# Routing's intermediates in the PSUM bank of the logits, and some of routing's copies on ScalarE, in an attention and mixture-of-experts kernel

## The chip, the cores and the metric

The kernel runs on one core of a Trainium2 chip. The core has five engines that run side by side, each through its own list of instructions in order: TensorE (PE in the profile; PEld are its weight loads), VectorE (DVE), ScalarE (ACT), GpSimd (POOL) and SyncE (SP), which here issues most of the DMAs. They hand work to each other through semaphores. There are two on-chip memories of 128 partitions: SBUF, and PSUM with eight banks, into which TensorE writes its results. The metric is the device time of one execution in microseconds. Lower is better.

## The reference

An attention over 64 heads (8 batches of 8 heads, 576 tokens, head size 64) that keeps only the keys whose score lies within `tau` of the row's maximum, followed by a mixture of 8 experts, of which each token uses the one with the largest logit:

```python
scores = scale * np.matmul(q, k.transpose(0, 1, 3, 2))
thresh = np.max(scores, axis=-1, keepdims=True) - tau
scores = np.where(scores >= thresh, scores, -1000000000.0)
attn = np.exp(scores - np.max(scores, axis=-1, keepdims=True))
attn = attn / (np.sum(attn, axis=-1, keepdims=True) + 1e-09)
x = np.matmul(attn, v)            # then (4608 tokens, 512)
logits = x @ w_gate               # (4608, 8)
expert_idx = np.argmax(logits, axis=1)
probs = softmax(logits)           # with 1e-09 added to the sum
out[n] = probs[n, e] * (np.maximum(x[n] @ w1[e], 0.0) @ w2[e])   # e = expert_idx[n]
```

## The kernel before, in words

The heads are worked on in 32 pairs, four pairs to a batch. For each pair the scores are computed twice: once with queries on the partitions (`s_unit`), where VectorE takes the row maxima out of PSUM (L288), and once with keys on the partitions (`st_unit`), with the threshold of each row already subtracted by TensorE (the operand CQ, L325). ScalarE takes the exponential of the second (L341), VectorE masks it by the sign of the score (L344), ScalarE casts it to 16 bits (L349) and GpSimd computes the remainder of that cast (L350). The product with the values follows (`av_piece`). All numbers go through TensorE as pairs of 16-bit values, high and low part; the low parts of queries and keys are made by L209, those of the values by L243, both on VectorE.

The row maxima of a pair go through TensorE as a transpose (L299, the tile pst), are split into three 16-bit rows (L304 to L307, the tile ptT) and are copied by DMA into CQ (L312).

When the four pairs of a batch are done, `finish` divides by the row sums (rs: L422, L423, for the half-filled tile of odd batches also L427, L428), GpSimd multiplies (L437), and the 16-bit rows are written into R, the rows that will be sent to the experts. `logits` has TensorE compute the logits (the tile lg). VectorE adds their high and low parts into the SBUF tile L (L470), and `route` works on that: the maximum mx, a one-hot oh of the first largest expert by way of w, rank8 and mw, and the difference ex. The nested `ranks` has TensorE count in a second tile rk, by two triangular matmuls, how many tokens of this and the earlier batches go to the same expert; VectorE makes of it the row posi to which each token is sent (L517, L520, L522, L524), and of ex the weight of its expert (L519 to L525). `run` holds the counts so far, `was` its copy from before this batch, `tid` the tokens' numbers. GpSimd sends each row of R by an indirect DMA (L534) to the table xs in HBM. The experts fetch their rows from xs, and TensorE computes them (L777, L804), for the most part after the attention.

Three things set the order of the work. A planner in the code counts steps, eleven to a pair of heads, and runs functions at a step and at one of three places in it, FRONT, MID and END; `after(k, f)` plans f k steps later, and `chain(k, fs)` spreads a list of functions over MID and END of successive steps. The tile framework then puts every engine's instructions into a fixed list, by readiness and the order of the program, with a timeline of its own (`schedule_with_timeline_sim=True`). And tiles are taken from pools: a tile of a pool with one buffer is given out again only when every reader of the last one is done. This one matters here:

```python
ps_m = ctx.enter_context(tc.tile_pool(name="ps_m", bufs=1, space=bass.MemoryType.PSUM))   # L67
ps = ps_m.tile([P, 512], F32, tag="m", name=f"pst_{n}")    # the transposes of the row maxima
lg = ps_m.tile([P, 512], F32, tag="m", name=f"lg_{b}")     # the logits
rk = ps_m.tile([P, 512], F32, tag="m", name=f"rk_{b}")     # the ranks
pc = ps_m.tile([P, 512], F32, tag="m", name=f"pc_{nm}")    # the counts for the tables, three times
```

All four share one bank of PSUM, one after the other. The logits use 64 or 80 of its 512 columns, the ranks 32 or 40.

The functions that the diff touches:

Of the kernel before, what the change touches and what calls it, by code (L numbers as in the profile page):

```python
# [50 lines left out]
def kernel(  # L51
# [355 lines left out]

    R = rpool.tile([P, 5, ROW], I32, name="R")
    Rf = R.bitcast(F32)
    L = rpool.tile([P, 5, E], F32, name="L")  # L410


    def finish(b):
        x = str(b) if b >= B - 3 else ""
        gap, lag, dist = (TUNE[z + x] for z in "gld")
        off = TUNE["off" + x] if b < B - 1 else 2
        n = NT + b % 2
        x4, xh = x_tiles(b)
        rs = small.tile([P, 5, H], F32, tag="rs", name=f"rs_{b}", bufs=2)
        eps = 1e-9 * SV / SX  # L420
        fs = [
            lambda: nc.vector.tensor_scalar(rs[:, 0:NT].unsqueeze(3), x4[:, :, :, D:W], eps, None, ALU.add),  # L422
            lambda: nc.vector.reciprocal(rs[:, 0:NT], rs[:, 0:NT]),  # L423
        ]
        if n > NT:
            fs += [
                lambda: nc.vector.tensor_scalar(rs[:, NT].unsqueeze(2), xh[:, :, D:W], eps, None, ALU.add),  # L427
                lambda: nc.vector.reciprocal(rs[:, NT], rs[:, NT]),  # L428
            ]
        chain(0, fs)  # L430
        xTs = {}

        def one(j):
            xr = x4[:, j] if j < NT else xh
            x = xp.tile([P, DM], F32, tag="xn", name=f"xn_{b}_{j}", bufs=2).rearrange("p (h d) -> p h d", h=H)
            eng = nc.vector if (b, j) in XV else nc.gpsimd
            eng.tensor_tensor(  # L437
                x, xr[:, :, 0:D], rs[:, j].unsqueeze(2).to_broadcast([P, H, D]), ALU.mult
            )
            x = x.rearrange("p (c u) d -> p c (u d)", c=4)  # L440
            Rv = R[:, j, 0:DM].bitcast(F16).rearrange("p (c h d) -> p c h d", c=4, h=2)

            def high():
                nc.scalar.copy(Rv[:, :, 0, :], x)
                eng.tensor_tensor(Rv[:, :, 1, :], x, Rv[:, :, 0, :], ALU.subtract)
                after(lag, turn)

            def turn():
                if j % 2 == 0:
                    xTs["t"] = rpool.tile([P, 2, 8, P], F16, tag="xT", name=f"xTg_{b}_{j}", bufs=3)  # L450
                xTs[j] = xT = xTs["t"][:, j % 2]
                nc.sync.dma_start_transpose(xT, R[:, j, 0:DM].bitcast(F16))

            after(lag, high)

        for j in range(n):
            after(off + gap * j, lambda j=j: one(j))
        after(off + gap * (n - 1) + 2 * lag + TUNE["lg7" if b == B - 1 else "lg"], lambda: logits(b, n, xTs, dist))

    def logits(b, n, xTs, dist):  # L460
        lg = ps_m.tile([P, 512], F32, tag="m", name=f"lg_{b}")
        lv = lg[:, 0:n * 2 * E].rearrange("p (j h e) -> p j h e", j=n, h=2)
        seq = [(0, 0)] + [(c, 1) for c in range(4)] + [(c, 0) for c in range(1, 4)]
        for j in range(n):
            for m, (c, h) in enumerate(seq):
                nc.tensor.matmul(
                    lv[:, j, 0:2 - h], xTs[j][:, 2 * c + h, :], wg[:, c, 0:2 - h, :],
                    start=(m == 0), stop=(m == 7),
                )
        after(1, lambda: nc.vector.tensor_reduce(  # L470
            L[:, 0:n, :], lv.rearrange("p j h e -> p j e h"), axis=AX.X, op=ALU.add
        ), FRONT)
        after(TUNE["route"], lambda: route(b, n, dist))

    def route(b, n, dist):

        Lj = L[:, 0:n, :]
        bc = [P, n, E]

        def t3(nm, dt=F32):  # L480
# [2 lines left out]
        def t2(nm, dt=F32):  # L483
            return small.tile([P, 5, 1], dt, tag=nm, name=f"{nm}_{b}", bufs=2)[:, 0:n, :]

        tt = nc.vector.tensor_tensor
        mx, w, mw, oh, ex, ps, pos, sm = (
            t2("mx"), t3("w"), t2("mw"), t3("oh", F16), t3("ex"), t3("ps"), t2("pos"), t2("sm")
        )
        was = small.tile([P, E], F16, tag="was", name=f"was_{b}", bufs=2)  # L490
        got = small.tile([P, E], F32, tag="got", name=f"got_{b}", bufs=2)
        posi = small.tile([P, 5], I32, tag="posi", name=f"posi_{b}", bufs=2)
# [2 lines left out]
            lambda: tt(w, Lj, mx.to_broadcast(bc), ALU.is_equal),  # L495
            lambda: tt(ex, Lj, mx.to_broadcast(bc), ALU.subtract),
            lambda: tt(w, w, rank8.unsqueeze(1).to_broadcast(bc), ALU.mult),
            lambda: nc.vector.tensor_copy(was, run),
            lambda: nc.vector.tensor_copy(
                R[:, 0:n, DM + 1:DM + 2], tid[:, b // 2, 4 * (b % 2):4 * (b % 2) + n].unsqueeze(2)  # L500
            ),
            lambda: nc.vector.tensor_reduce(mw, w, axis=AX.X, op=ALU.max),
            lambda: tt(oh, w, mw.to_broadcast(bc), ALU.is_equal),
            lambda: nc.vector.tensor_reduce(got, oh.rearrange("p j e -> p e j"), axis=AX.X, op=ALU.add),
            lambda: tt(run, run, got, ALU.add),
        ])

        def ranks():
            nc.scalar.activation(ex, ex, AF.Exp, scale=1.0 / (SX * SG))
            rk = ps_m.tile([P, 512], F32, tag="m", name=f"rk_{b}")  # L510
            rkv = rk[:, 0:n * E].rearrange("p (j e) -> p j e", e=E)
            for j in range(n):
                nc.tensor.matmul(rkv[:, j], before, oh[:, j], start=True, stop=False)
                for i in range(j):
                    nc.tensor.matmul(rkv[:, j], ones, oh[:, i], start=False, stop=False)
                nc.tensor.matmul(rkv[:, j], ones, was, start=False, stop=True)
            after(1, lambda: tt(ps, rkv, base_e.unsqueeze(1).to_broadcast(bc), ALU.add), FRONT)  # L517
            fs = [
                lambda: nc.vector.tensor_reduce(sm, ex, axis=AX.X, op=ALU.add),  # L519
                lambda: tt(ps, ps, oh, ALU.mult),  # L520
                lambda: nc.vector.tensor_scalar(sm, sm, 1e-9, None, ALU.add),
                lambda: nc.vector.tensor_reduce(pos, ps, axis=AX.X, op=ALU.add),  # L522
                lambda: nc.vector.reciprocal(sm, sm),
                lambda: nc.vector.tensor_copy(posi[:, 0:n].unsqueeze(2), pos),  # L524
                lambda: nc.vector.tensor_scalar(  # L525
                    Rf[:, 0:n, DM:DM + 1], sm, 1.0 / (SX * SW * SW), None, ALU.mult
                ),
            ]
            if b == 0:
                fs.append(lambda: nc.vector.tensor_copy(pos0, pos[:, 0]))  # L530
            chain(1, fs)

            def send(j):
                nc.gpsimd.indirect_dma_start(  # L534
                    xs[:, :], bass.IndirectOffsetOnAxis(ap=posi[:, j:j + 1].bitcast(U32), axis=0), R[:, j, :], None
                )
                sent.add((b, j))

            if b in TABLES:
                after(6 + dist * n, TABLES[b])  # L540
            for j in range(n):
                after(6 + dist * j, lambda j=j: send(j))
# [593 lines left out]
```

## Time and profile before

| | |
|---|---|
| median of three runs | 1108.96 us (1107.15 to 1111.02) |
| the profiled execution | 1107.99 us |
| its span, from the first to the last instruction | 1105.5 us |
| TensorE busy | 950.0 us, 86% |
| VectorE busy | 793.7 us, 72% |
| ScalarE busy | 646.7 us, 59% |
| GpSimd busy | 574.5 us, 52% |
| mean granted clock of TensorE | 0.947 of full speed |

In the rows shown below, a group stands as line, engine, operation, output tile and input tiles, their partitions x elements and types, the number of instructions, then busy time in us and the mean duration of one in ns, then the time that the engine sat idle just before them and what ended it. A row of the timeline begins with start and length in us. "mean" and "busy" hold everything between an instruction's start and its end, also a time in which it stood still.

### The profile page before, as it was taken

How to read it: one execution, taken by the hardware profiler on the slowest of the kernel's cores; microseconds unless marked ns; L12 is line 12 of the kernel's file. 1: busy time of each engine (PE TensorE's matmuls, PEld its weight loads, DVE VectorE, ACT ScalarE, POOL GpSimd, SP SyncE). 2: the span in 40 equal slices, each digit the busy share in tenths (PEclk: the TensorE clock that was granted, in tenths of full speed). 3: DMA queues.
4: the chain of work that ended last, by engine and by line, in shares of the span. 5: the costliest groups of instructions: out<-in, count | busy, mean ns of one | idle time of the engine just before them, and what ended most of it. 6: DMA issues, size and time to landing. Idle time of an engine off the chain costs nothing.

```text
span 1105.5 us, 26826 instructions
## 1 busy us (share of the span) xinstructions
PE 950.0 (86%) x10699; PEld 616.1 (56%) x10699; DVE 793.7 (72%) x1385; ACT 646.7 (59%) x1030; POOL 574.5 (52%) x459
## 2 busy tenths in 40 slices
PE   3888799698979698887798669888999999999996
PEld 1345465355545365544464348556866766766784
DVE  8889999899989899999999984471534334334460
ACT  2688788687867687776787555441524324334551
POOL 2367775975976876875976864224212222222221
PEclk9899899989989899999999769889999999999998
DMA  6554544554545363544443434985957557547620
GB/s 193 139 153 110 130 100 113 116 125 118 133 102 151 106 147 99 122 122 125 92 100 110 122 68 102 299 273 124 299 163 219 148 166 203 160 148 226 208 98 24
DMA packets 142555, 159.06 MB, mean 144 GB/s; under 512 B 96345, under 2 KB 112731, under 8 KB 142428
## 3 DMA queue, kind: packets, MB, share of 16 engines
q1 hardware_dynamic: 133276, 127.88, 44.5%
q0 software_dynamic: 9152, 29.45, 8.1%
q8 instruction: 85, 1.39, 0.5%
q14 instruction: 42, 0.34, 0.1%
HBM read 90.24 MB, written 19.44 MB: 99 GB/s over the span
## 4 chain that ended last, share of the span: by engine, by line
PE 45%; DVE 26%; DMA 11%; issue 10%; ACT 4%; POOL 2%; SPq 2%; POOLq 0%; DVEq 0%; ACTq 0%
PE h L777 15%; PE y L804 13%; DVE nm L288 7%; DVE e L344 6%; PE st L324 3%; PE s L276 3%; DVE lo L209 3%; PE st L325 3%; PE s L278 2%; DMA out_dram<-o,gt 2%; DVE vop L243 2%; DMA xs<-R,posi 2%; DMA CQ<-hi 2%; PE av L390 2%; PE av L391 1%
## 5 line engine op out<-in xcount | busy, mean ns | idle before, releaser
L350 POOL TENSOR_TENSOR pl<-e,ph 128x1024 f16<-128x1024 f32 x158 | 344.4, 2184 | 167.4 <-ACT ph L349 128.5
L341 ACT ACTIVATE e<-st,ntau 128x512 f32<-128x512 f32 (+1 forms) x352 | 218.9, 647 | 37.7 <-PE st L325 35.3
L344 DVE SCALAR_TENSOR_TENSOR e<-st,e 128x512 f32<-128x512 f32 (+1 forms) x352 | 216.6, 631 | 8.3 <-ACT e L341 7.9
L288 DVE TENSOR_REDUCE nm<-s 128x1 f32<-128x512 f32 x320 | 199.1, 630 | 19.7 <-PE s L278 18.4
L777 PEld LDWEIGHTS <-wb 128*128 128x128 f16 x2304 | 192.2, 100 | 26.7 <-issue 5.0
L777 PE MATMUL h<-xTm,wb 128*128 128x256 f16 (+2 forms) x2112 | 199.5, 257 | 8.5 <-DMA xTm<-R 8.5
L804 PE MATMUL y<-wb,hl 128*128 128x512 f16 (+1 forms) x1056 | 203.6, 362 | 0.0
L276 PE MATMUL s<-QK 128*128 128x512 f16 (+3 forms) x640 | 145.3, 305 | 67.0 <-DVE nm L288 37.8
L349 ACT CAST ph<-e 128x1024 f16<-128x1024 f32 x160 | 166.4, 1040 | 49.8 <-DVE e L344 49.6
L324 PE MATMUL st<-QK 128*128 128x512 f16 (+3 forms) x640 | 146.2, 305 | 46.3 <-DVE nm L288 27.9
L390 PE MATMUL av<-vop,pl 128*128 128x65 f16 (+1 forms) x1280 | 161.8, 197 | 3.2 <-POOL pl L350 3.1
L389 PE MATMUL av<-vop,ph 128*128 128x64 f16 (+1 forms) x1280 | 161.5, 197 | 0.6 <-ACT ph L349 0.6
L391 PE MATMUL av<-vop,ph 128*128 128x65 f16 (+1 forms) x1280 | 161.9, 197 | 0.0
L696 DVE SCALAR_TENSOR_TENSOR wb<-wf,wb 128x1024 f16<-128x1024 f32 x96 | 122.6, 1313 | 47.9 <-ACT wb L695 47.6
L804 PEld LDWEIGHTS <-hl 128*128 128x128 f16 (+1 forms) x1056 | 94.6, 100 | 99.5 <-issue 4.0
L325 PE MATMUL st<-CQ,ck 128*128 128x512 f16 (+3 forms) x640 | 144.1, 301 | 2.3 <-DMA CQ<-ptT 2.3
L278 PE MATMUL s<-ck,CQ 128*128 128x512 f16 (+3 forms) x640 | 144.0, 301 | 0.0
L390 PEld LDWEIGHTS <-pl 128*128 128x128 f16 (+1 forms) x1280 | 123.0, 102 | 26.1 <-issue 8.5
L391 PEld LDWEIGHTS <-ph 128*128 128x128 f16 (+1 forms) x1280 | 123.2, 102 | 23.2 <-issue 10.8
L389 PEld LDWEIGHTS <-ph 128*128 128x128 f16 (+1 forms) x1280 | 123.6, 102 | 22.1 <-issue 10.5
L816 POOL DMA_INDIRECT out_dram<-o,gt x40 | 44.8, 1120 | 142.7 <-ACT o L815 123.5
L765 ACT ACTIVATE hl<-h 128x512 f16<-128x512 f32 (+1 forms) x80 | 45.6, 573 | 123.0 <-PE h L777 120.9
(183 smaller groups left out, 1221.5 us busy)
## 6 DMA issues: line engine op xcount, KB each, us to landing
wf<-in_w_dram SPq DMA_DIRECT2D x96, 512.0 KB
qkf<-in_qk_dram SPq DMA_DIRECT2D x32, 576.0 KB
vf<-in_v_dram SPq DMA_DIRECT2D x16, 640.0 KB
QK<-hi SPq DMA_DIRECT2D x64, 144.0 KB
QK<-hi SPq DMA_DIRECT2D x64, 72.0 KB
QK<-lo SPq DMA_DIRECT2D x64, 72.0 KB
ck<-lo SPq DMA_DIRECT2D x64, 72.0 KB
CQ<-hi SPq DMA_DIRECT2D x64, 64.0 KB
```

The source lines that it names most:

```text
L276: nc.tensor.matmul(sc[rows, oc], d["QA"][a][:, cols], d["KB"][a][:, CH[c]], start=True, stop=False)
L288: nc.vector.tensor_reduce(o, sc[:, 0:width(t)], axis=AX.X, op=ALU.max, negate=True)
L324: nc.tensor.matmul(sc[rows, oc], d["KB"][a][:, cols], d["QA"][a][:, CH[c]], start=True, stop=False)
L325: nc.tensor.matmul(sc[rows, oc], d["CK"][a][:, cols], d["CQ"][:, q], start=False, stop=True)
L341: nc.scalar.activation(pf, sc, AF.Exp, bias=ntau, scale=0.125 / SS)
L344: nc.vector.scalar_tensor_tensor(pf, sc, 0.0, pf, ALU.is_ge, ALU.mult)
L350: (nc.vector if (n, t) in PLV else nc.gpsimd).tensor_tensor(l, pd, h, ALU.subtract)
L389: nc.tensor.matmul(av[rows, a, 0:D], h, vop[:, tv, W:W + D], start=False, stop=False)
L390: nc.tensor.matmul(av[rows, a], l, vop[:, tv, 0:W], start=False, stop=False)
L391: nc.tensor.matmul(av[rows, a], h, vop[:, tv, 0:W], start=False, stop=a == 1 and i >= 2 and j == NT - 1)
L777: nc.tensor.matmul(o, Wt[:, c, wh, f], x, start=c == 0 and z == 0, stop=c == 3 and z == 2,)
L804: nc.tensor.matmul(o, h[:, hh], Wt[:, f, wh, c], start=f == 0 and z == 0, stop=f == 7 and z == 2)
```

## The change: what it does

Routing's intermediates move from SBUF into free columns of the PSUM bank that holds the logits (L becomes Lj, and w) or the ranks (ps, pos, and the sum total). Five steps move from VectorE to ScalarE: the two additions of eps to the row sums, the copies `was` and R<-tid, and the scaling that writes the weight into R. In the list of `route` the two copies also move behind oh. The tiles mx, mw, oh, ex, sm, was, got and posi stay in SBUF.

```diff
-    L = rpool.tile([P, 5, E], F32, name="L")
 def finish(b):
-            lambda: nc.vector.tensor_scalar(rs[:, 0:NT].unsqueeze(3), x4[:, :, :, D:W], eps, None, ALU.add),
+            lambda: nc.scalar.activation(rs[:, 0:NT].unsqueeze(3), x4[:, :, :, D:W], AF.Copy, bias=eps),
             lambda: nc.vector.reciprocal(rs[:, 0:NT], rs[:, 0:NT]),
-                lambda: nc.vector.tensor_scalar(rs[:, NT].unsqueeze(2), xh[:, :, D:W], eps, None, ALU.add),
+                lambda: nc.scalar.activation(rs[:, NT].unsqueeze(2), xh[:, :, D:W], AF.Copy, bias=eps),
 def logits(b, n, xTs, dist):
+        Lj, w = (lg[:, z:z + n * E].rearrange("p (j e) -> p j e", e=E) for z in (128, 192))
         after(1, lambda: nc.vector.tensor_reduce(
-            L[:, 0:n, :], lv.rearrange("p j h e -> p j e h"), axis=AX.X, op=ALU.add
+            Lj, lv.rearrange("p j h e -> p j e h"), axis=AX.X, op=ALU.add
         ), FRONT)
 def route(b, n, dist, Lj, w):
-        Lj = L[:, 0:n, :]
-        mx, w, mw, oh, ex, ps, pos, sm = (
-            t2("mx"), t3("w"), t2("mw"), t3("oh", F16), t3("ex"), t3("ps"), t2("pos"), t2("sm")
-        )
+        mx, mw, oh, ex, sm = t2("mx"), t2("mw"), t3("oh", F16), t3("ex"), t2("sm")
             lambda: tt(w, w, rank8.unsqueeze(1).to_broadcast(bc), ALU.mult),
-            lambda: nc.vector.tensor_copy(was, run),
-            lambda: nc.vector.tensor_copy(
+            lambda: nc.vector.tensor_reduce(mw, w, axis=AX.X, op=ALU.max),
+            lambda: tt(oh, w, mw.to_broadcast(bc), ALU.is_equal),
+            lambda: nc.scalar.copy(was, run),
+            lambda: nc.vector.tensor_reduce(got, oh.rearrange("p j e -> p e j"), axis=AX.X, op=ALU.add),
+            lambda: nc.scalar.copy(
                 R[:, 0:n, DM + 1:DM + 2], tid[:, b // 2, 4 * (b % 2):4 * (b % 2) + n].unsqueeze(2)
             ),
-            lambda: nc.vector.tensor_reduce(mw, w, axis=AX.X, op=ALU.max),
-            lambda: tt(oh, w, mw.to_broadcast(bc), ALU.is_equal),
-            lambda: nc.vector.tensor_reduce(got, oh.rearrange("p j e -> p e j"), axis=AX.X, op=ALU.add),
             lambda: tt(run, run, got, ALU.add),
 def ranks():
+            ps = rk[:, 64:64 + n * E].rearrange("p (j e) -> p j e", e=E)
+            pos, total = (rk[:, z:z + n].unsqueeze(2) for z in (128, 136))
             after(1, lambda: tt(ps, rkv, base_e.unsqueeze(1).to_broadcast(bc), ALU.add), FRONT)
-                lambda: nc.vector.tensor_reduce(sm, ex, axis=AX.X, op=ALU.add),
+                lambda: nc.vector.tensor_reduce(total, ex, axis=AX.X, op=ALU.add),
                 lambda: tt(ps, ps, oh, ALU.mult),
-                lambda: nc.vector.tensor_scalar(sm, sm, 1e-9, None, ALU.add),
+                lambda: nc.vector.tensor_scalar(sm, total, 1e-9, None, ALU.add),
                 lambda: nc.vector.tensor_reduce(pos, ps, axis=AX.X, op=ALU.add),
                 lambda: nc.vector.reciprocal(sm, sm),
                 lambda: nc.vector.tensor_copy(posi[:, 0:n].unsqueeze(2), pos),
-                lambda: nc.vector.tensor_scalar(
-                    Rf[:, 0:n, DM:DM + 1], sm, 1.0 / (SX * SW * SW), None, ALU.mult
-                ),
+                lambda: nc.scalar.activation(Rf[:, 0:n, DM:DM + 1], sm, AF.Copy, scale=1.0 / (SX * SW * SW)),
```

More of the change, by code (lines that the diff above doesn't have):

```diff
@@ L469, in logits, with route @@
                 )
+        Lj, w = (lg[:, z:z + n * E].rearrange("p (j e) -> p j e", e=E) for z in (128, 192))
         after(1, lambda: nc.vector.tensor_reduce(
-            L[:, 0:n, :], lv.rearrange("p j h e -> p j e h"), axis=AX.X, op=ALU.add
+            Lj, lv.rearrange("p j h e -> p j e h"), axis=AX.X, op=ALU.add
         ), FRONT)
-        after(TUNE["route"], lambda: route(b, n, dist))
-    def route(b, n, dist):
-        Lj = L[:, 0:n, :]
+        after(TUNE["route"], lambda: route(b, n, dist, Lj, w))
+    def route(b, n, dist, Lj, w):
         bc = [P, n, E]
```

## The prediction

> **What bounds the kernel now.** I read the busy time by engine first, then the same in three stretches, then the groups of VectorE's instructions, and last the timeline and the chain of waits around the longest of them. The page and the three stretches (columns: stretch, its length, busy time and count of each engine, granted TensorE clock, DMA share, GB/s):
>
> ```profile
> span 1105.5 us, 26826 instructions
> PE 950.0 (86%) x10699; PEld 616.1 (56%) x10699; DVE 793.7 (72%) x1385; ACT 646.7 (59%) x1030; POOL 574.5 (52%) x459
> ...
> 100.00:610.00 510.00, 427.67 (x5844) 259.98 (x5843) 481.13 (x827) 384.52 (x651) 378.36 (x233) 0.95 0.47 117
> 610.00:750.00 140.00, 110.29 (x1416) 79.25 (x1415) 95.66 (x213) 69.67 (x109) 70.42 (x58) 0.84 0.62 171
> 750.00:1105.00 355.00, 341.76 (x2664) 239.19 (x2662) 130.47 (x174) 132.84 (x176) 81.13 (x107) 0.99 0.58 169
> ```
>
> There are two kernels in one. From 750 us on, TensorE is busy 342 of 355 us and nothing of the change is there. From 100 to 610 us, the attention, VectorE is busy 481 of 510 us (94%), TensorE 428 (84%), ScalarE 385 (75%), GpSimd 378 (74%). What the change is worth is read in that stretch, and there VectorE sets the pace. Its groups, edited lines first, then neighbours (busy us, mean ns; idle before):
>
> ```profile
> L499 DVE COPY R<-tid 128x4 int32<-128x4 int32 (+1 forms) x8 | 18.4, 2306 | 1.5 <-DMA xs<-R,posi 1.5
> L497 DVE TENSOR_TENSOR w<-w,rank 128x32 f32<-128x32 f32 (+1 forms) x8 | 8.7, 1089 | 0.0
> L498 DVE COPY was<-run 128x8 f16<-128x8 f16 x8 | 5.1, 633 | 0.0
> L520 DVE TENSOR_TENSOR ps<-ps,oh 128x32 f32<-128x32 f32 (+1 forms) x8 | 4.6, 580 | 0.0
> L521 DVE TENSOR_SCALAR sm<-sm 128x4 f32<-128x4 f32 (+1 forms) x8 | 4.6, 572 | 0.0
> L422 DVE TENSOR_SCALAR rs<-x 128x32 f32<-128x32 f32 x8 | 4.3, 540 | 0.0
> L524 DVE CAST posi<-pos 128x4 int32<-128x4 f32 (+1 forms) x8 | 4.1, 516 | 0.0
> L495 DVE TENSOR_TENSOR w<-L,mx 128x32 f32<-128x32 f32 (+1 forms) x8 | 4.0, 496 | 0.1
> L503 DVE TENSOR_TENSOR oh<-w,mw 128x32 f16<-128x32 f32 (+1 forms) x8 | 3.9, 491 | 0.0
> L525 DVE TENSOR_SCALAR R<-sm 128x4 f32<-128x4 f32 (+1 forms) x8 | 2.0, 252 | 0.0
> L427 DVE TENSOR_SCALAR rs<-xh 128x8 f32<-128x8 f32 x4 | 0.6, 162 | 0.0
> L517 DVE TENSOR_TENSOR ps<-rk,base_e 128x32 f32<-128x32 f32 (+1 forms) x8 | 1.4, 175 | 0.0
> L496 DVE TENSOR_TENSOR ex<-L,mx 128x32 f32<-128x32 f32 (+1 forms) x8 | 1.5, 187 | 0.0
> L209 DVE SCALAR_TENSOR_TENSOR lo<-qkf,hi 128x1152 f16<-128x1152 f32 (+1 forms) x33 | 67.4, 2044 | 14.0 <-ACT hi L206 13.4 <-DMA CQ<-hi 0.4
> L243 DVE SCALAR_TENSOR_TENSOR vop<-vf,vop 128x640 f16<-128x640 f32 x32 | 36.9, 1155 | 0.6 <-ACT vop L242 0.6
> L505 DVE TENSOR_TENSOR run<-run,got 128x8 f16<-128x8 f16 x8 | 4.9, 615 | 0.0
> ```
>
> A copy of five numbers per partition (L499) takes 2.3 us in the mean, where an instruction on 40 numbers (L517) takes 0.175. The timeline says why, VectorE first, then GpSimd (start, length):
>
> ```profile
> 541.37 3.37 DVE L499 COPY R<-tid 128x5 int32<-128x5 int32 x1
> ...
> 542.59 2.11 POOL L350 TENSOR_TENSOR pl<-e,ph 128x1024 f16<-128x1024 f32 x1
> ...
> 365.82 8.43 DVE L499 COPY R<-tid 128x5 int32<-128x5 int32 x1
> 375.02 1.34 DVE L209 SCALAR_TENSOR_TENSOR lo<-qkf,hi 128x1152 f16<-128x1152 f32 x1
> ...
> 364.82 2.13 POOL L350 TENSOR_TENSOR pl<-e,ph 128x1024 f16<-128x1024 f32 x1
> ...
> 373.19 1.03 POOL L437 TENSOR_TENSOR xn<-x,rs 128x512 f32<-128x512 f32 x1
> ...
> 193.51 0.80 DVE L243 SCALAR_TENSOR_TENSOR vop<-vf,vop 128x640 f16<-128x640 f32 x1
> ```
>
> The copy of 541.37 ends at 544.74, GpSimd's instruction at 544.70. The copy of 365.82 ends at 374.25, when six GpSimd instructions without a gap between them (364.82 to 374.22) end. The last row is L243 undisturbed, as that of 375.02 is L209. So the time is a stall behind GpSimd. It befalls instructions that take two tensors, or a copy, cast or scaling, from SBUF to SBUF. L517, which reads one input from PSUM, has none. L496, with both inputs in SBUF, has none either, but it runs right behind L495, on which the wait has fallen by then.
>
> **The change part by part.**
>
> *The stalls.* Five edited lines leave VectorE: 18.4 + 5.1 + 4.3 + 2.0 + 0.6 = 30.4 us; without stall their 36 instructions are worth 36 x 0.16 (L427) = 5.8. Six stay and get a PSUM input: 8.7 + 4.6 + 4.6 + 4.1 + 4.0 + 3.9 = 29.9, and 48 x 0.175 (L517) = 8.4 without stall. The stalls are 24.6 + 21.5 = 46 us, and VectorE loses 52 of 794 us. What of it sets the end is read from the chain of waits (start, length, what):
>
> ```profile
> 178.69 1.08 DVE w L495
> ...
> 366.42 1.25 issue
> 367.78 6.38 issue
> ...
> 657.50 1.84 DVE oh L503
> ```
>
> Of its 195 longest pieces 17 lie on edited lines, the first and the last shown, 31.0 us together; less 17 x 0.17 of own work, 28.1. The two "issue" pieces lie under the 8.43 us copy: 7.6. So 35.7 of the 46 us are on the path. The moved instructions' own 5.8 us are worth nothing to 5.8; half, 3, since small ones overlap their neighbours. Gain so far 38.7.
>
> *Where a stall goes.* L209, L243 and L505 keep two SBUF inputs. A GpSimd run that stalled an edited instruction is still running if one of them comes soon after. After the copy of 365.82 comes L209, 0.77 us later: without the copy it starts at 366.6 and waits until 374.2, so 7.5 of the 8.3 us only change owner. Followed likewise through the timeline for all 28 stalls, 12.9 us of the 46 change owner. Bounds 0 and 12.9; I take 12.9, since GpSimd's order does not change.
>
> *PSUM in place of SBUF.* Thirteen instructions per batch get a PSUM operand. Reading costs nothing by L517 against L496. Writing: the rows below, the upper with input and output in PSUM, the lower with output in SBUF, differ by 0.07 us:
>
> ```profile
> L305 DVE SCALAR_TENSOR_TENSOR pst<-pst,thr,ptT 9x128 f32<-9x128 f32 x32 | 10.8, 338 | 0.0
> L307 DVE TENSOR_TENSOR ptT<-pst,ptT 9x128 f16<-9x128 f32 x32 | 8.5, 267 | 1.2 <-ACT ptT L306 1.2
> ```
>
> Seven writes per batch, 56 in all, cost nothing to 3.9 us; I take 2, as the operations of the two rows differ too. The Trainium skill speaks against the change here: Perfetto Trace Analysis, section Optimizing Scalar/DVE Operations, gives a VectorE instruction some 60 ns of overhead on SBUF and 125 on PSUM, reads included. By it the 104 instructions of eight batches would cost 6.8 us (estimate from that page), and the sum would come out 5 us later; L517 against L496 does not bear that out for reads.
>
> *ScalarE.* It gets 36 instructions. The nearest row:
>
> ```profile
> L509 ACT ACTIVATE ex<-ex 128x32 f32<-128x32 f32 (+1 forms) x8 | 1.8, 228 | 0.8 <-DVE ex L496 0.7
> ```
>
> 36 x 0.23 = 8.3 us on an engine that is 75% busy: 0 to 8.3. Two waits are added: the copy of tid into R waits, as L499 did for 1.5 us in all, until the batch before has left R, and behind it on ScalarE stand the exponentials (L341), for which VectorE's masks wait; and the reciprocal of rs waits for ScalarE. I take 1. The scatter's queue on GpSimd waits for the scaling on ScalarE instead of VectorE, at no cost: in all eight batches L525 ran before the cast of the positions, L524, for which the scatter waits too. In the planner's list mw and oh move one step forward and the two copies behind them; that too I take as nothing, since the framework orders VectorE's list by readiness anyway.
>
> *The bank.* The pool of tag "m" has one bank. The logits now hold it until oh (L503), not until L470; the ranks until posi (L524), not until L517. The transposes pst (L299) of the row maxima need the same bank:
>
> ```profile
> 188.18 0.28 PE L299 MATMUL pst<-ident,r 128*9 128x128 f32 x1
> 192.78 0.15 DVE L524 CAST posi<-pos 128x4 int32<-128x4 f32 x1
> ...
> 505.70 0.27 PE L299 MATMUL pst<-ident,r 128*9 128x128 f32 x1
> 513.86 0.15 DVE L524 CAST posi<-pos 128x4 int32<-128x4 f32 x1
> 523.34 0.38 PE L325 MATMUL st<-CQ,ck 128*128 128x512 f16 x1
> ```
>
> At seven places the transpose ran before the instant at which the bank will be free: by 4.7, 1.0, 2.2, 1.6, 2.3, 8.3 and 2.9 us, 23.0 together (the first and the largest are shown). Behind a waiting transpose stand TensorE's score tiles, and on SyncE the loads queued behind the copies of ptT into CQ. Its rows are needed by the first L325 of that pair of heads, at 523.34, 17.6 us after the transpose of 505.70, so most of a delay is covered, and the stalls that delay posi get shorter. Bounds 0 and 23.0; I take 2, near the low end.
>
> *Sum.* -38.7 + 12.9 + 2 + 1 + 2 = -20.8. The profiled execution took 1107.99 us (its span of 1105.5 and 2.5 around it): 1087.2. The median, 1108.96, stands 1 us above it, so 1088.2; I say 1087, between the two.
>
> **The rivals.** (a) Nothing changes owner and the extras are hidden: -38.7, 1069. For it: the order of VectorE's list is drawn anew and may keep L209 out of GpSimd's long runs. Against it: L209 and L243 stall already (their means stand 0.7 and 0.35 us above their undisturbed rows).
> (b) The waits close up: with VectorE freed, GpSimd is fed faster, its 74% grows, and the remaining two-SBUF instructions, which stall (67.4 - 33 x 1.34) + (36.9 - 32 x 0.80) + (4.9 - 8 x 0.16) = 38 us today, take most of it over. With 20 us in place of 12.9 moved, and TensorE's 84% leaving half of the rest: -(38.7 - 20) / 2 + 5 = -4, 1104.
> (c) The change doesn't do what it says: an instruction with a PSUM output still stalls. Then only the moved ones count, five of the 17 pieces of the chain, 10.4 us, and the 7.6, of which 7.5 change owner: about -10, 1098. Against it: L517.
> (d) Slower, by the bank alone: each of the seven delays stops TensorE in order, and does so again at L325 because the rows come late by as much, less some 2 to 5 us of cover each: 23 + 14 = 37, against 20.8 + 2 of gain: +14, 1122. It decides once the waits for the bank cost over 23 us, 3.3 at a place. Against it: 17.6 us stand between transpose and first use in the rows above. For it: TensorE's order is fixed beforehand, by estimates that know nothing of the stalls.
>
> **How the numbers follow.** Forecast 0.55 (1076 to 1098 by its own bounds), (a) 0.14, (b) 0.12, (c) 0.05, (d) 0.14. The range takes in (a) nearly and (b): 1068 to 1108, leaving out most of (d). A measurement here tells 0.3%, 3.3 us, from no change: faster 0.78 (the forecast, (a), (c) and a third of (b)), same 0.08, slower 0.14.
>
> **What would show it.** In the groups of the changed kernel, the six edited lines that stay must stand at 0.15 to 0.25 us with no member over 0.4; the moved ones at 0.2 to 0.3 on ScalarE. L209's and L243's means tell how much changed owner: 2.4 us for L209 would be all 12.9 on that line, 2.04 + 12.9 / 33. From 100 to 610 us the stage must end some 20 us earlier at about the same share of VectorE. TensorE idling before L299 or L325 with VectorE's posi or oh, or a DMA into CQ, as the releaser shows (d). Were the stage as long as before with the small instructions at 0.18, the reading of the path would be wrong.

## The result and the profile after

The changed kernel takes 1081.66 us (median of 4 runs, 1071.95 to 1083.73), the kernel before, run beside it, 1108.37 us (4 runs, 1107.15 to 1111.02). The ratio is 0.9745, with a 95% interval from 0.9697 to 0.9794: faster by 27 us. The execution that was profiled took 1083.73 us.

The line numbers of the changed kernel are one smaller than before in `finish` (L422 is L421) and two smaller in `route` (L495 is L493; oh, moved in its list, goes from L503 to L497). In `ranks` they are the same, and behind it two smaller again (L572 is L570). First the page of the changed kernel:

```profile
span 1082.0 us, 26826 instructions
...
PE 939.5 (87%) x10699; PEld 607.0 (56%) x10699; DVE 748.3 (69%) x1349; ACT 650.6 (60%) x1066; POOL 580.4 (54%) x459
```

VectorE has 36 instructions fewer and is busy 45.4 us less (793.7 before); ScalarE has the 36, and 3.9 us more. The groups of VectorE and ScalarE that answer to those of before (busy us, mean ns; idle before):

```profile
L493 DVE TENSOR_TENSOR lg<-lg,mx 128x32 f32<-128x32 f32 (+1 forms) x8 | 1.6, 197 | 0.1
L495 DVE TENSOR_TENSOR lg<-lg,rank 128x32 f32<-128x32 f32 (+1 forms) x8 | 1.6, 197 | 0.1
L497 DVE TENSOR_TENSOR oh<-lg,mw 128x32 f16<-128x32 f32 (+1 forms) x8 | 1.5, 188 | 0.0
L520 DVE TENSOR_TENSOR rk<-rk,oh 128x32 f32<-128x32 f32 (+1 forms) x8 | 1.5, 190 | 0.0
L521 DVE TENSOR_SCALAR sm<-rk 128x4 f32<-128x4 f32 (+1 forms) x8 | 1.2, 146 | 0.0
L524 DVE CAST posi<-rk 128x4 int32<-128x4 f32 (+1 forms) x8 | 1.2, 153 | 0.0
L517 DVE TENSOR_TENSOR rk<-rk,base_e 128x32 f32<-128x32 f32 (+1 forms) x8 | 1.5, 187 | 0.1
L494 DVE TENSOR_TENSOR ex<-lg,mx 128x32 f32<-128x32 f32 (+1 forms) x8 | 1.5, 187 | 0.1
L209 DVE SCALAR_TENSOR_TENSOR lo<-qkf,hi 128x1152 f16<-128x1152 f32 (+1 forms) x33 | 65.9, 2001 | 17.9 <-ACT hi L206 17.8
L243 DVE SCALAR_TENSOR_TENSOR vop<-vf,vop 128x640 f16<-128x640 f32 x32 | 37.5, 1176 | 1.8 <-ACT vop L242 1.8
L503 DVE TENSOR_TENSOR run<-run,got 128x8 f16<-128x8 f16 x8 | 6.8, 850 | 0.1
L570 DVE TENSOR_SCALAR lim<-cnt 128x8 f32<-128x8 f32 x3 | 7.1, 2355 | 0.0
L421 ACT ACTIVATE rs<-x 128x32 f32<-128x32 f32 x8 | 2.0, 246 | 0.0
L500 ACT COPY R<-tid 128x4 int32<-128x4 int32 (+1 forms) x8 | 1.6, 198 | 1.0 <-issue 1.0
```

The upper six rows are the six edited lines that stay on VectorE: together 8.6 us where they took 29.9. The longest single member of the six is 0.21 us, where the means alone were 0.49 to 1.09 before.

Second, the stage of the attention, from the start of the span to the end of the last product with the values, in both kernels (stretch, length, busy time and count of PE, PEld, DVE, ACT, POOL, granted clock, DMA share, GB/s). Before:

```profile
0.00:684.90 684.90, 552.42 (x7436) 337.40 (x7437) 623.68 (x1106) 486.64 (x817) 475.01 (x334) 0.93 0.47 119
```

After:

```profile
0.00:655.50 655.50, 542.14 (x7436) 328.58 (x7437) 577.40 (x1074) 490.46 (x851) 479.01 (x335) 0.96 0.48 125
```

The stage is 29.4 us shorter. VectorE's busy time in it falls by 46.3 us; its idle time, length less busy, rises from 61.2 to 78.1. In two more profiles of the same kernel the stage takes 661.9 and 656.2 us, with VectorE busy 579.5 and 576.3. The mean of the three is 27.0 us less than before: 45.9 us of busy time gone, 18.9 of idle time come. The rest of the span was 5.9, 1.8 and -1.9 us longer than before's 420.6. So the gain was made in the attention, and what comes behind it neither gives nor takes.

The view of waits tells where VectorE's idle time is (who waits, for whom: us in total, times, longest). Before:

```profile
DVE nm L288 <- PE s L278: 18.4, 24, 2.6
DVE lo L209 <- ACT hi L206: 13.4, 10, 2.4
DVE e L344 <- ACT e L341: 7.9, 10, 2.4
...
PE st L325 <- DMA CQ<-ptT: 2.3, 2, 1.5
```

After:

```profile
DVE nm L288 <- PE s L278: 23.6, 35, 2.7
DVE lo L209 <- ACT hi L206: 17.8, 15, 4.5
DVE e L344 <- ACT e L341: 13.7, 15, 6.0
DVE pst L305 <- ACT ptT L304: 4.6, 3, 3.4
...
PE st L325 <- DMA CQ<-ptT: 6.7, 4, 2.2
```

VectorE catches up with TensorE's scores, with ScalarE's casts and its exponentials; and TensorE waits three times as long as before for the thresholds (ptT) to arrive in CQ.

Why they arrive late is seen at the tenth pair of heads, first before, then after (the row maxima r; posi, behind which the ranks leave the bank; the transpose, which before began at 188.18, as the prediction shows):

```profile
182.63 0.16 DVE L295 TENSOR_REDUCE r<-nm 128x9 f32<-128x18 f32 x1
...
176.41 0.16 DVE L295 TENSOR_REDUCE r<-nm 128x9 f32<-128x18 f32 x1
190.81 0.15 DVE L524 CAST posi<-rk 128x4 int32<-128x4 f32 x1
191.12 0.28 PE L299 MATMUL pst<-ident,r 128*9 128x128 f32 x1
```

The transpose begins 5.4 us after its maxima are ready before, and 14.6 us after them in the changed kernel, just behind posi. TensorE doesn't stand still meanwhile: it is busy 12.9 of these 14.6 us with other work. Summed over the 32 pairs, the time from the end of L295 to the start of L299 is 34.7 us before and 96.0 in the changed kernel (95.2 and 97.5 in its other two profiles); the largest pieces are 14 to 20 us, at the pairs 10, 18 and 26.

In the profiled execution 5.9 us of the 29.4 were lost again behind the attention. The timeline shows the largest piece (start, length):

```profile
759.58 0.15 DVE L733 COPY gt<-R 128x1 f32<-128x1 f32 x1 [12.03 <-DMA out_dram<-o,gt]
759.72 4.63 DVE L694 SCALAR_TENSOR_TENSOR wb<-wf,wb 128x1024 f16<-128x1024 f32 x4
764.27 3.08 DVE L764 SCALAR_TENSOR_TENSOR hl<-h,hl 128x512 f16<-128x512 f32 x5
765.01 3.23 PE L802 MATMUL y<-wb,hl 128*128 128x512 f16 x8 [4.06 <-DVE hl L764]
```

A small copy waits 12 us for a transfer; four instructions of L694 and five of L764 stand behind it in VectorE's order, and TensorE waits 4.1 us for the last. In the other two profiles of the changed kernel the copy waits 10.3 and 9.9 us and TensorE 2.0, so the 4.1 us are no steady cost.

### The profile page after: what moved, and what is told of

The parts are those of the page before. It is cut to its first block, busy times and chain, and to the rows that moved or that the text cites. A ratio compares the mean times of both kernels' runs of the same rounds, so it can differ in the third digit from the quotient of the medians.

```text
span 1082.0 us, 26826 instructions
## 1 busy us (share of the span) xinstructions
PE 939.5 (87%) x10699; PEld 607.0 (56%) x10699; DVE 748.3 (69%) x1349; ACT 650.6 (60%) x1066; POOL 580.4 (54%) x459
## 4 chain that ended last, share of the span: by engine, by line
PE 41%; DVE 21%; DMA 15%; issue 11%; SPq 5%; ACT 4%; POOL 4%; POOLq 0%; DVEq 0%; ACTq 0%
PE h L775 13%; PE y L802 11%; DVE nm L288 5%; DVE e L344 5%; DMA CQ<-hi 3%; PE st L324 3%; PE s L276 3%; DVE lo L209 3%; DMA out_dram<-o,gt 3%; PE st L325 2%; PE s L278 2%; DVE vop L243 2%; DMA wf<-in_w_dram 2%; POOL pl L350 2%; DVE wb L694 1%
## 5 line engine op out<-in xcount | busy, mean ns | idle before, releaser
L341 ACT ACTIVATE e<-st,ntau 128x512 f32<-128x512 f32 (+1 forms) x352 | 217.0, 647 | 31.5 <-PE st L325 29.9
L344 DVE SCALAR_TENSOR_TENSOR e<-st,e 128x512 f32<-128x512 f32 (+1 forms) x352 | 216.2, 633 | 14.2 <-ACT e L341 13.7
L276 PE MATMUL s<-QK 128*128 128x512 f16 (+3 forms) x640 | 142.3, 300 | 50.0 <-DVE nm L288 20.7
L324 PE MATMUL st<-QK 128*128 128x512 f16 (+3 forms) x640 | 143.1, 300 | 30.6 <-DVE e L344 18.5
L390 PE MATMUL av<-vop,pl 128*128 128x65 f16 (+1 forms) x1280 | 158.4, 196 | 5.7 <-POOL pl L350 5.6
L389 PE MATMUL av<-vop,ph 128*128 128x64 f16 (+1 forms) x1280 | 158.2, 196 | 2.5 <-ACT ph L349 2.5
L391 PE MATMUL av<-vop,ph 128*128 128x65 f16 (+1 forms) x1280 | 159.0, 196 | 0.0
L694 DVE SCALAR_TENSOR_TENSOR wb<-wf,wb 128x1024 f16<-128x1024 f32 x96 | 118.5, 1274 | 51.8 <-ACT wb L693 51.8
L325 PE MATMUL st<-CQ,ck 128*128 128x512 f16 (+3 forms) x640 | 139.0, 296 | 6.7 <-DMA CQ<-ptT 6.7
L278 PE MATMUL s<-ck,CQ 128*128 128x512 f16 (+3 forms) x640 | 140.7, 295 | 0.0
L389 PEld LDWEIGHTS <-ph 128*128 128x128 f16 (+1 forms) x1280 | 122.3, 101 | 21.2 <-issue 7.6
L391 PEld LDWEIGHTS <-ph 128*128 128x128 f16 (+1 forms) x1280 | 121.9, 101 | 19.7 <-issue 9.0
L693 ACT ACTIVATE wb<-wf 128x1024 f16<-128x1024 f32 x96 | 97.6, 1049 | 39.4 <-DMA wf<-in_w_dram 16.9
```

The costliest lines, as they stand in the source:

```text
L276: nc.tensor.matmul(sc[rows, oc], d["QA"][a][:, cols], d["KB"][a][:, CH[c]], start=True, stop=False)
L324: nc.tensor.matmul(sc[rows, oc], d["KB"][a][:, cols], d["QA"][a][:, CH[c]], start=True, stop=False)
L341: nc.scalar.activation(pf, sc, AF.Exp, bias=ntau, scale=0.125 / SS)
L344: nc.vector.scalar_tensor_tensor(pf, sc, 0.0, pf, ALU.is_ge, ALU.mult)
L389: nc.tensor.matmul(av[rows, a, 0:D], h, vop[:, tv, W:W + D], start=False, stop=False)
L390: nc.tensor.matmul(av[rows, a], l, vop[:, tv, 0:W], start=False, stop=False)
```

## The experiments

My theory: small VectorE instructions with two SBUF inputs, or copies and scalings from SBUF to SBUF, wait behind GpSimd's instructions; the change takes 84 such instructions out of the way, and the time of the kernel follows. Rivals: that only the moves to ScalarE, or only the PSUM, do it; that VectorE's load as such, not the stall, is what counts; that the bank, held longer, takes part of the gain; and that the stalls just change owner.

**Half of the change: the moves alone.** The kernel before, with the five instructions on ScalarE, in the order of the changed list, all intermediates in SBUF:

```diff
-lambda: nc.vector.tensor_scalar(rs[:, 0:NT].unsqueeze(3), x4[:, :, :, D:W], eps, None, ALU.add),
+lambda: nc.scalar.activation(rs[:, 0:NT].unsqueeze(3), x4[:, :, :, D:W], AF.Copy, bias=eps),
 ...                       # the same for rs[:, NT]
-lambda: nc.vector.tensor_copy(was, run),
-lambda: nc.vector.tensor_copy(R[:, 0:n, DM + 1:DM + 2], tid[...]),
 lambda: nc.vector.tensor_reduce(mw, w, ...), lambda: tt(oh, w, ...),
+lambda: nc.scalar.copy(was, run),
 lambda: nc.vector.tensor_reduce(got, oh...),
+lambda: nc.scalar.copy(R[:, 0:n, DM + 1:DM + 2], tid[...]),
 ...
-lambda: nc.vector.tensor_scalar(Rf[:, 0:n, DM:DM + 1], sm, 1.0 / (SX * SW * SW), None, ALU.mult),
+lambda: nc.scalar.activation(Rf[:, 0:n, DM:DM + 1], sm, AF.Copy, scale=1.0 / (SX * SW * SW)),
```

> Only the five moves to ScalarE; the intermediates stay in SBUF, so the bank is held as before. Stall theory (a meeting with GpSimd costs an edited instruction about 0.55 us in the mean, and some 55% of VectorE's freed time reaches the end): VectorE loses 30 of the 52 us of the sum, the end comes 13 to 18 us earlier, 1090 to 1096. The six lines that stay keep means of 0.5 to 1.1 us. Rival, change of owner: L209, L243 and L505 take over the stall of the copies (their busy time, 109 us before, rises by 7 or more), and the gain is under 8 us. Rival, the PSUM half alone does it: no gain.

Measured: 1085.41 us (1084.29 to 1089.48) against 1107.53, ratio 0.9788 [0.9733, 0.9843], 22 us less, more than the 13 to 18 expected. Stage and two groups of it:

```profile
0.00:663.80 663.80, 541.65 (x7436) 333.98 (x7437) 599.38 (x1073) 490.86 (x850) 480.44 (x334) 0.96 0.48 123
...
L521 DVE TENSOR_SCALAR sm<-sm 128x4 f32<-128x4 f32 (+1 forms) x8 | 9.2, 1146 | 0.0
L497 DVE TENSOR_TENSOR w<-w,rank 128x32 f32<-128x32 f32 (+1 forms) x8 | 6.2, 770 | 0.0
```

VectorE is busy 768.3 us in all, 25.4 less than before, and idles 64.4 us of the stage, 3 more than before: nearly all that was freed reached the end. The six lines that stay in SBUF still take 28.1 us together (29.9 before), but not the same ones stall: L521 takes 1146 ns in place of 572, while oh, with both inputs in SBUF as before, takes 184 ns in place of 491. Which instruction meets GpSimd is dealt out anew when the order of the list changes.

**The other half: PSUM alone.** The changed kernel, with the five instructions back on VectorE at their new places in the list:

```diff
-lambda: nc.scalar.copy(was, run),
+lambda: nc.vector.tensor_copy(was, run),
 ...                       # likewise R <- tid, both rs, and the scaling
```

> Only the intermediates in PSUM; the copies, the eps and the scaling stay on VectorE. Stall theory: the six lines fall to 0.15 to 0.2 us each, VectorE loses some 20 us, the end comes 8 to 13 us earlier, 1095 to 1100, and the moved lines keep 30 us. Rival, the bank: if the longer hold costs 5 us or more, under 5 us is left of the gain, 1103 or later. Rival, PSUM does not free them: their means stay at 0.5 to 1.1.

Measured: 1096.27 us (1093.33 to 1098.66), ratio 0.9868 [0.9814, 0.9921], 11 us less.

```profile
0.00:674.80 674.80, 546.89 (x7435) 332.91 (x7436) 594.54 (x1091) 486.55 (x818) 478.73 (x332) 0.93 0.48 121
...
L500 DVE COPY R<-tid 128x4 int32<-128x4 int32 (+1 forms) x8 | 11.9, 1486 | 3.2 <-DMA xs<-R,posi 3.1
L495 DVE TENSOR_TENSOR lg<-lg,rank 128x32 f32<-128x32 f32 (+1 forms) x8 | 1.6, 195 | 0.1
```

The six lines run at 144 to 195 ns, the copies go on stalling. VectorE is busy 768.0 us, freed by as much as with the moves alone, but half of the gain arrives: its idle time in the stage is 80.3 us, 19 more than before. The transposes wait 81.4 us for their start behind the row maxima, 39.3 with the moves alone. Moves and PSUM by themselves give 22 and 11, together 33; the change has 26 to 27. So both do something. The intervals reach some 6 us to either side of each half, so it is not shown that together they are more than the whole; but the PSUM half leaves VectorE waiting, and the moves don't.

**A hold of the bank that did not hold.** The kernel before, with a small reduction that reads the bank, written behind oh and behind posi. It was meant to keep the bank taken for as long as in the changed kernel:

```diff
-lambda: tt(oh, w, mw.to_broadcast(bc), ALU.is_equal),
+lambda: (tt(oh, w, mw.to_broadcast(bc), ALU.is_equal),
+         nc.vector.tensor_reduce(hold, lg[:, 0:E], axis=AX.X, op=ALU.max)),
 ...                       # likewise behind posi, from rk
```

> The kernel before, with the bank held as long as in the changed one: 16 small reductions read it behind oh and behind posi (some 1.5 us of own work). Prediction's term: 2 us for the hold, 1110 to 1113 in all. Rival, the bank matters: in the changed kernel the pairs that follow the ranks of an even batch come 25 to 29 us after the pair before, where 17 is usual; then 8 us or more, 1116 or later, and the gaps between the first L325 of successive pairs grow behind batches 0, 2 and 4.

Measured: 1107.32 us (1101.63 to 1109.48, 10 runs), ratio 0.9986 [0.9952, 1.002]: no difference. The profile is of the shortest of the ten:

```profile
0.00:676.20 676.20, 554.05 (x7434) 337.77 (x7435) 614.52 (x1104) 488.28 (x817) 475.29 (x332) 0.94 0.47 121
...
188.50 0.18 DVE L519 TENSOR_TENSOR ps<-rk,base_e 128x32 f32<-128x32 f32 x1
188.60 0.15 DVE L527 TENSOR_REDUCE hold<-rk 128x1 f32<-128x8 f32 x1
190.87 0.40 PE L299 MATMUL pst<-ident,r 128*9 128x128 f32 x1
195.15 0.15 DVE L526 CAST posi<-pos 128x4 int32<-128x4 f32 x1
```

The reductions read nothing that oh or posi writes, and the framework put all sixteen directly behind the old last reader of the bank, as here behind L519. So the bank comes free some 0.1 us later than before and not 7 us later, the transpose runs ahead of posi, and the transposes wait 42.1 us in all, about as long as before (34.7). The run tells nothing of what the hold costs. It does tell something else: with sixteen small reductions added, VectorE is busy 787.9 us, 5.8 less than before, so the stalls differ by that much when the list changes a little.

**The changed kernel again**, on the chip of these three, as the control:

> The changed kernel again, as the measure for the others: 1072 to 1084, since one of its four times so far was 1072 and three 1081 to 1084. If the short time is a matter of the mixture of experts, where VectorE's copy gt waited 12 us for a DMA and held TensorE for 4.1, a short run shows a wait of under 7 us there.

1082.45 us (1076.63 to 1086.27), ratio 0.9735 [0.9672, 0.9797]. The profiled execution was a long one (1086.27 us). The short one that was profiled later (1076.67) shows a wait of the copy gt of 9.9 us, not under 7, so that wait is not what makes an execution short.

**The ranks earlier.** The changed kernel, with the ranks of three batches three steps earlier in the planner, to take them away from a transpose:

```diff
-after(TUNE["ranks"], ranks)
+after(4 if b in (0, 2, 4) else TUNE["ranks"], ranks)
```

> The changed kernel with ranks three planner steps earlier in batches 0, 2 and 4, so that posi is done before the transpose of the row maxima asks for the bank. If the bank costs what the prediction said (2 us), 1079 to 1083. Rival, the bank costs 8 us or more: 1065 to 1075, and the first L325 of the pairs behind those batches come under 22 us after the one before.

Measured: 1078.13 us (1075.98 to 1083.52), ratio 0.973 [0.9662, 0.9798], the same as the changed kernel. But the pairs behind these batches start as far apart as before the edit (26.1, 23.8 and 30.7 us from one first L325 to the next; 25.4, 23.5 and 29.3 in the changed kernel), and the transposes wait 95.5 us as there: the planner's step didn't move the work. This run tells nothing of the bank.

**A dose of the stall, and of the work without it.** The changed kernel, with 96 more instructions on two numbers, three in a pair of heads, once as a copy from SBUF to SBUF, once as a reduction of the same two numbers:

```diff
+if t in (1, 4, 7):
+    nc.vector.tensor_copy(dose, nm[:, 0, t - 1:t + 1])                                        # the first
+    nc.vector.tensor_reduce(dose[:, 0:1], nm[:, 0, t - 1:t + 1], axis=AX.X, op=ALU.max)       # the second
```

> The changed kernel with 96 copies of two numbers from SBUF to SBUF added on VectorE, three to a pair of heads, behind row maxima 1, 4 and 7; nobody reads them. Stall theory: each costs 0.15 us and a stall of 0.55 in the mean, VectorE is busy 60 to 70 us longer, and 45 to 60% of that reaches the end: 1108 to 1122. Rival, change of owner: L209 and L243 give back what the copies take, VectorE's busy time rises by under 30 us and the end comes under 15 us later.

> The same with reductions in place of the copies: same count, same place, same two numbers, but no stall expected. Stall theory: 96 x 0.15, busy 8 to 15 us longer, the end 3 to 8 us later: 1084 to 1090. Rival, it is the number of instructions and not the stall behind GpSimd: the same time as with the copies.

With the copies 1137.86 us (1136.86 to 1149.11), ratio to the kernel before 1.0299 [1.0217, 1.038]. Stage and groups:

```profile
0.00:714.70 714.70, 567.82 (x7440) 343.21 (x7441) 646.02 (x1170) 495.71 (x851) 476.63 (x335) 0.91 0.45 114
...
L291 DVE COPY dose<-nm x96: 146/601/8079, 20.4 to 657.1; 128x2 f32<-128x2 f32 x96
...
L291 DVE COPY dose<-nm 128x2 f32<-128x2 f32 x96 | 102.3, 1066 | 0.2
L210 DVE SCALAR_TENSOR_TENSOR lo<-qkf,hi 128x1152 f16<-128x1152 f32 (+1 forms) x33 | 53.4, 1620 | 9.4 <-ACT hi L207 8.5 <-DMA CQ<-ptT 0.8
```

With the reductions 1095.57 us (1091.39 to 1099.72), ratio 0.9896 [0.9833, 0.9959]:

```profile
0.00:670.20 670.20, 550.99 (x7435) 335.59 (x7436) 580.37 (x1169) 491.46 (x850) 480.05 (x334) 0.94 0.47 122
...
L291 DVE TENSOR_REDUCE dose<-nm x96: 123/142/157, 20.5 to 610.9; 128x1 f32<-128x2 f32 x96
```

(The middle row of the first and the last of the second give the shortest, the median and the longest in ns.) The same number of instructions on the same two numbers at the same places costs 42 us more as a copy than as a reduction. The reductions take 0.14 us each and never more than 0.157; the copies take 0.146 at the least and up to 8.08. This is the price of the stall itself: of 88.9 us (102.3 less 13.4 of the reductions) 42 arrive at the end. Of the 96 copies 64 take over 0.3 us, and each of these ends 0.02 to 0.04 us after an instruction of GpSimd ends; the 27 edited instructions of the kernel before that took over 0.3 us likewise end within 0.06 us of one. The Trainium skill gives the mechanism: in SBUF — State Buffer, section Who interferes with whom, it says that VectorE's copies, casts and scalings can take the port pair that it shares with GpSimd, and instructions with two SBUF inputs contend with GpSimd's reads, while reductions on trn2, and instructions with at most one SBUF input outside those modes, never contend. The two doses agree, and so do the six rows at 146 to 197 ns.

Both doses cost more than I had expected. The run with the reductions takes 13 us longer than the control above, 17 longer than the run with the ranks earlier, which was on the same chip and is the changed kernel in all that matters. But that isn't their 13.4 us of work arriving in full: small instructions overlap their neighbours, and VectorE is busy only 2.8 us more in the stage than in the run with the ranks earlier (580.4 and 577.6), while it idles 8.9 us more (89.8 and 80.9) and TensorE waits 10.8 us for the thresholds in place of 6.9. Why the waits grow is not shown.

**A longer hold, and a stall less.** In the changed kernel got still lies in SBUF, so the sum into run stalls (L503, 850 ns). Here it lies in the bank of the logits as well:

```diff
-after(TUNE["route"], lambda: route(b, n, dist, Lj, w))
+after(TUNE["route"], lambda: route(b, n, dist, Lj, w, lg[:, 256:256 + E]))     # got
```

> The changed kernel with got, too, in the bank of the logits, so that the sum run + got has one input in SBUF. Stall theory: that line falls from 6.8 us to 1.4, the end comes 2 to 4 us earlier, 1077 to 1081. Rival, the bank: it is held one step longer by the logits, which in the odd batches meets the transpose, and the time does not fall or rises.

Measured: 1090.41 us (1090.0 to 1096.41), ratio 0.9853 [0.9787, 0.992], 8 us slower than the control (12 than the run with the ranks earlier, on its chip), although the sum into run falls from 6.8 to 1.2 us and VectorE to 743.7 us.

```profile
0.00:667.40 667.40, 552.11 (x7436) 335.65 (x7437) 572.50 (x1075) 491.00 (x850) 480.23 (x336) 0.94 0.48 123
...
PE st L325 <- DMA CQ<-ptT: 14.2, 7, 4.2
```

VectorE has lost another 5 us of work in the stage and idles 94.9 us; TensorE waits 14.2 us for the thresholds. The transposes wait 125.3 us in all, 96 in the changed kernel, now also behind odd batches (8.5 us at pair 15, 7.0 at pair 23, where it was 2.1 and 2.9). Here the longer hold of the bank costs more than the stall that it saves.

**A shorter hold.** The changed kernel, with the bank of the ranks free after one instruction: the counts are multiplied by the one-hot straight out of PSUM into SBUF; the expert's first row comes as a ninth column, made from mw by ScalarE; the cast to posi and the eps on the sum are on ScalarE too:

```diff
-ps = rk[:, 64:64 + n * E]...; pos, total = (rk[:, z:z + n].unsqueeze(2) for z in (128, 136))
-after(1, lambda: tt(ps, rkv, base_e.unsqueeze(1).to_broadcast(bc), ALU.add), FRONT)
+after(1, lambda: tt(ps[:, :, 0:E], rkv, oh, ALU.mult), FRONT)          # ps, pos in SBUF
 ...
+nc.scalar.activation(ps[:, :, E:E + 1], mw, AF.Copy, scale=-float(CAP), bias=float(E * CAP))
-lambda: nc.vector.tensor_scalar(sm, total, 1e-9, None, ALU.add),
+lambda: nc.scalar.activation(sm, sm, AF.Copy, bias=1e-9),
-lambda: nc.vector.tensor_copy(posi[:, 0:n].unsqueeze(2), pos),
+lambda: nc.scalar.copy(posi[:, 0:n].unsqueeze(2), pos),
```

> The changed kernel with the bank of the ranks free again after one instruction, as before the change: VectorE multiplies the ranks by oh straight out of the bank into SBUF, the first row of the expert comes from ScalarE as a ninth column, and the positions are the sum over nine columns; the cast and the eps go to ScalarE. VectorE has 24 small instructions less (some 3 us). Bank theory (the longer hold costs the changed kernel 8 us or more, since the row maxima come late into CQ): 1066 to 1075, TensorE's wait for CQ<-ptT falls from 6 to 7 us to under 3, and the pair behind batches 0, 2 and 4 follows within 22 us instead of 24 to 30. Rival, the bank costs 2 us as predicted: 1077 to 1081.

And the same with run as one reduction over the one-hots and the old counts, which lie side by side in one tile, in place of got and the sum:

```diff
-lambda: nc.vector.tensor_reduce(got, oh.rearrange("p j e -> p e j"), axis=AX.X, op=ALU.add),
-lambda: tt(run, run, got, ALU.add),
+lambda: nc.vector.tensor_reduce(run, ohw[:, 0:n + 1].rearrange("p j e -> p e j"), axis=AX.X, op=ALU.add)
```

> The same, with the counts made by one reduction over oh and was in place of got and the sum run + got. Stall theory: the 6 to 8 us of that line go, VectorE loses some 7 us, the end comes another 3 to 6 us earlier. Rival, change of owner: L209 and L243 take it over and the time stays.

The changed kernel beside these two:

> The changed kernel once more beside the two: 1077 to 1086, 0.974 of the kernel before.

The shorter hold takes 1080.85 us (1078.57 to 1085.36, 6 runs; ratio 0.9737 [0.9692, 0.9783]), with the one reduction 1082.93 (1078.85 to 1087.48, 6 runs; 0.9763 [0.9716, 0.9809]), the changed kernel 1083.48 (1076.67 to 1088.32, 6 runs; 0.9764 [0.9716, 0.9812]). The three can't be told apart, where 1066 to 1075 had been expected of the shorter hold. Its rows:

```profile
0.00:654.20 654.20, 542.26 (x7436) 332.52 (x7437) 589.26 (x1051) 492.79 (x871) 480.00 (x334) 0.94 0.49 125
...
L243 DVE SCALAR_TENSOR_TENSOR vop<-vf,vop 128x640 f16<-128x640 f32 x32 | 44.5, 1392 | 0.0
L694 DVE SCALAR_TENSOR_TENSOR wb<-wf,wb 128x1024 f16<-128x1024 f32 x96 | 128.8, 1380 | 49.4 <-ACT wb L693 48.4 <-issue 0.5
...
PE st L325 <- DMA CQ<-ptT: 1.3, 1, 1.3
```

The waits went as expected: the transposes wait 49.6 us in all, TensorE hardly waits for the thresholds, the pairs behind batches 0, 2 and 4 follow after 20.4, 17.4 and 16.8 us, and VectorE's idle time in the stage is 64.9 us, close to the 61.2 of before. But VectorE is busy 589.3 us where the control is busy 576.3: L243 takes 44.5 us (38.6 in the control) and L694 128.8 (117.8), of which 24.4 against 12.9 in the stage. These are instructions with two SBUF inputs, longer with the same work. With the one reduction for run (its line falls from 6.8 to 1.8 us) the stage ends at 649.0 us, 7 earlier than the control, and the kernel no earlier: its last batch's logits come at 679 to 681 us in both, since, by the code, from the attention's end each step of `finish` and `logits` waits for the one before, and the experts wait for that.

## Why the prediction was right, and where it was not

The time was forecast as 1087 us, 1068 to 1108, and is 1081.66: a gain of 27 us where 21 were forecast.

**The sum as it stands.** The seventeen pieces of the chain add up to 29.0 us and not to 31.0, so that 33.7 us of the stalls lie on the path and the sum is -18.8, 1089. The forecast's own bounds, added up, reach from some 1066 to 1120, wider than the 1076 to 1098 that were given. In (d), the 14 us of a second wait don't follow from 2 to 5 us of cover at each of the seven places, which leave 10 at the most. None of this moves the forecast out of its range.

**The reading of the bound** held. VectorE sets the pace of the attention, and the time that its small instructions spend behind GpSimd is what the change removes. The tests that were promised came out: six lines at 146 to 197 ns with no member over 0.21 us, the moved ones at 195 to 246 ns on ScalarE. With this rival (c), that PSUM doesn't free an instruction, has fallen. VectorE loses on the edited lines 30.4 + 21.3 = 51.7 us, 52 by the prediction.

**Where a stall goes** is the step that failed. It gave 12.9 us back to L209, L243 and the sum into run, "since GpSimd's order does not change". Those three took 109.2 us before; in the three profiles of the changed kernel they take 110.2, 112.3 and 110.4, in that of the moves alone 110.5, and with PSUM alone 102.5. In the run whose hold did not hold, with sixteen small reductions added and nothing else, they took 105.2, so differences of some us come with a new order alone. L209's mean, forecast to tell, is 2.0 us and not 2.4. Over all lines but the edited ones VectorE's busy time rose by 6.3 us (51.7 less 45.4), and 3.1 of that are on lim (L570, 4.0 before), which the step had not looked at. That stalls do change owner is seen in other runs: the copies' dose took 12.5 us off L209, and with the short hold L243 and L694 take 17.3 us more in the stage (5.8 and 11.5). But which instruction meets GpSimd can't be read by sliding one instruction along the old timeline. The runs suggest that the order of all engines shifts with every stall that goes, but none of them isolates this.

**How the 6 us between forecast and measurement arise.** By the prediction VectorE is freed of 37 us net (52 less 12.9 on other lines and 2 of writes) and waits 16.3 us more (the 13.3 of the 52 that it left off the path, and 3 for the bank and ScalarE). Measured in the stage are 45.9 us freed and 18.9 of new idle time, which leaves the 27.0 by which it ended earlier. So 9 us more were freed than forecast, which is in the main the term on owners, and the waits came out 2.6 us larger.

**The bank and ScalarE** were put at 3 us together, and no run isolates them. That the bank makes work wait is shown by the transposes: at the pairs 10, 18 and 31 of the changed kernel they begin 0.2 to 0.4 us behind the end of posi, and their waits, 34.7 us in all before, are 39.3 with the moves alone, 81.4 with PSUM alone, 96 in the changed kernel, 125.3 with the longer hold and 49.6 with the shorter. VectorE's idle time in the stage follows (61.2, 64.4, 80.3, 80, 94.9 and 64.9), and the longer hold was 8 to 12 us slower with less work. So the place and the chain of the delay were foreseen: bank, transpose, CQ, L325. Its size at the transposes was not, 61 us more, with what follows on at the next pairs, where the bounds ended at 23.0; but TensorE has other work in its list at that place, and its wait at L325 grew by only 4.4 us. What the bank costs the changed kernel at the end is not settled: with a shorter hold the idle time went, the stalls on other lines came, and the end stayed. It may be that a VectorE that isn't waiting for TensorE is met by GpSimd more often; no run shows that.

**The writes to PSUM** were put at 2 us. L517, whose output went from SBUF to PSUM, takes 187 ns where it took 175; L494 (L496 before), of which an input went from SBUF to PSUM, takes 187 both times. At 0.012 us each, 56 writes are 0.7 us. The Trainium skill's figures (Perfetto Trace Analysis, section Optimizing Scalar/DVE Operations), by which an instruction on PSUM has some 65 ns more (estimate: the difference of its 125 and 60), do not show in these rows.

**The rivals.** (a), 1069, was too much in its sum, though right that no stall changes owner among the three lines. (b), that the waits close up, is true in a part: 19 of 46 us became waiting. But the three lines did not take over the stalls, and that was its condition. (d), slower by the bank, has fallen: its mechanism is there, 6.7 us of TensorE's wait for CQ in place of 2.3, but the 4.4 us more are a fifth of the 23 from which it would decide.

**The tail.** "Nothing of the change is there" from 750 us on is right for the median, and wrong for a single profile by up to 6 us, as the wait of 12 us above shows.

## What to carry to other kernels

A mean duration far above that of the shortest member of its group is a wait inside the instruction: compare it with a neighbour of the same size that reads from PSUM, or reduces, and look at what ends at the same instant on GpSimd. To be rid of such a wait, move the small instruction to an engine with room (here the cheaper half, 22 of 27 us), or let one operand stay in PSUM; then look at how long the bank is held, and at who else draws on it, for there the gain can be lost again (the longer hold here: 8 to 12 us). A stall that is removed may not be charged to the next instruction by the old timeline: sum the stalls of all lines of the new one instead.

## What was not expected of the hardware

A copy of two numbers per partition costs 1.07 us in the mean in this kernel, seven times its undisturbed 0.15, and 8.08 us at the most (the dose of copies). GpSimd is busy 477 of the 715 us of that stage, mostly in instructions of 1.0 to 2.2 us. The copy of 8.08 us, from 410.15 to 418.23, spans the end of one and six more behind it that follow without a gap to 418.19; the copy of 8.43 us in the kernel before lies over six in the same way.

TensorE's granted clock moved with the kernel: 0.93 in the stage before, 0.96 after, 0.91 with the copies' dose. Over whole runs it is 0.948 in the mean of 31 runs of the kernel before and 0.961 in 14 of the changed one, and within each kernel the shorter executions tend to have the higher clock. Whether a part of the gain comes by way of the clock, or the clock only follows from fewer interruptions, no run here tells apart; the two last variants reach the same time at 0.95, so the higher clock isn't needed for it.
